# A long-convolution gate and two expert layers on one core: weight steps moved later, layer 2 catching up with layer 1, ReLU groups in own banks, and half a transform in three fp32r passes

## The chip, the cores and the metric

The kernel runs on one core of one Trainium2 chip. The metric is the device time of one execution in microseconds (us), as the median of several runs; lower is better. The core has a matrix engine (TensorE, PE), three engines for elementwise work (VectorE = DVE, ScalarE = ACT, GpSimd = POOL), and a sync engine (SP) whose queue here issues most DMAs. Each engine runs its own program in order; semaphores make one wait for another.

## The reference, cut to what matters

```python
def _attn_ref(x, v, pos_emb, w1, w2):          # S = 12480, D = 128
    h_mlp = np.maximum(pos_emb @ w1, 0.0) @ w2
    h_filt = h_mlp * np.exp(-0.01 * np.arange(S))[:, None]
    u, L = x * v, 2 * S
    y = np.fft.irfft(np.fft.rfft(u, n=L, axis=1) * np.fft.rfft(h_filt, n=L, axis=0)[None], n=L, axis=1)[:, :S]
    return x * y

def _moe_ref(x, w_in, w_out):                  # 128 -> 2048 -> 128; the weights come as float64
    r = np.maximum(x @ w_in, 0.0)
    return (r * r) @ w_out

def _moe2_ref(x, w_in, w_out, alpha):
    h = x @ w_in
    return (np.maximum(h, 0.0) + alpha * np.minimum(h, 0.0)) @ w_out

# result: _moe2_ref of _moe_ref of _attn_ref
```

A long convolution (through a Fourier transform of twice the length) makes a gated sequence of 12480 tokens by 128 channels; two expert layers of 2048 hidden units follow, the first with a squared ReLU, the second with a ReLU whose negative side has a slope alpha for each unit.

## The kernel before, in words

**Stages.** The program is one order written out by hand; helper generators yield after each piece, and `run((a, n), (b, m))` interleaves two of them by their counts. In the order of time:

- `z_stage` (4 to 18 us): the filter's ReLU layer. Groups of up to four matmuls fill one PSUM bank (8 blocks of 64 columns, L192); the ReLU with the window factor is done by DVE for a whole group at once (L203) or by ACT block by block (L196). In some groups DVE takes the first half and ACT the second half of the same bank.
- `ar_stage` (19 to 46): the filter's first transform (L229, copies L231, sign flips L214).
- `u_stage(0)` interleaved with `r_stage` (46 to about 120): the signal's transform for the first half of the channels. `u_mm_a(k)` is the first transform (L287, 16 matmuls, two ACT copies L288 out of PSUM); `u_mm_b(k)` the second (L295, L296, L297, L300: four fp32 matmuls of 224 columns; ACT copies one bank at L299; DVE adds and subtracts at L303). There are 16 rounds k, and `u_mm_b(k - 1)` follows `u_mm_a(k)`. `r_stage` (L246, ACT L248, DVE L252 and L253) is the filter's second transform. GpSimd prepares the input of later rounds (L275, L214).
- `u_stage(1)` with `p_stage` (to 190), then the products and the inverse transform (`q0`, `b_stage`, `y_stage`, to 339.75). In these, steps of the weight decoding run beside the transforms.
- `moe` (339.75 to the end): both expert layers.

**Expert layers.** A table `seq` of 800 steps holds (layer, chunk of tokens, block t of 128 hidden units): 25 chunks (23 of 512 tokens, 2 of 352) by 16 blocks by 2 layers. At step k of one loop the program issues: `up(k)`, three fp32r matmuls into one of four banks (`mm3`, L582 to L584: high and low halves of both operands); `act(k)`, for layer 1 a ReLU on ACT (L602), for layer 2 either DVE's min times alpha (L607) or, at every third step, two ACT instructions (L604, L605); `mid(k - 1)` on DVE (L617), which reads the bank for the last time; `high(k - 2)`, ACT's cast to fp32r (L624); `low`, the remainder, on GpSimd, or on DVE at every fourth step (L635); and `down(k - 6)`, three more matmuls (L582 to L584 again) that add into the chunk's output bank. Layer 2 of a chunk needs all 16 steps of layer 1; its input is split into halves in `split_x`.

**Weights of layer 2.** They come as 64-bit words and are decoded in parts of two blocks. `decode` is a generator of 7 steps a part: load to `s_w` (L489, on SP's queue, three parts ahead), ACT (L495, L465), DVE or GpSimd (L453 to L470). `moe(back)` calls `next(back)` inside its loop, so each weight step is put into the engines' programs at one place of one step k. Weights decoded earlier come back from DRAM (`w_spill`) by POOL's queue into `w_o0b` and `w_i` (L775, L776).

Of the kernel before, what the change touches and what calls it, by code (L numbers as in the profile page):

```python
# [21 lines left out]
KA = HA + 1  # L22
# [36 lines left out]
def kernel(  # L59
# [122 lines left out]
        return w1_sb, win_sb  # L182

    def z_stage(w1_sb, win_sb):
        n_g = -(-HZ // 4)
        for g in range(n_g):
            j0 = 4 * g
            m = min(4, HZ - j0)
            n = min(2 * m, HB - 2 * j0)
# [3 lines left out]
            z = rv[:, :, 0, 2 * j0:2 * j0 + n]  # L193
            c = 0 if g in (1, 5, 9) else n // 2 if g in (3, 7, 11, 13) else n
            for i in range(c, n):
                nc.scalar.activation(  # L196
                    out=z[:, :, i],
                    in_=p[:, i],
                    func=ACTF.Relu,
                    scale=win_sb[:, 2 * j0 + i:2 * j0 + i + 1],  # L200
                )
            if c:
                nc.vector.scalar_tensor_tensor(  # L203
                    out=z[:, :, :c].rearrange("p f t -> p t f"),
                    in0=p[:, :c],
                    scalar=0.0,
                    in1=win_sb[:, 2 * j0:2 * j0 + c].unsqueeze(2).to_broadcast([NA, c, F]),
                    op0=ALU.max,
                    op1=ALU.mult,
                )  # L210
            yield

    def signed(eng, out, src, m):
        eng.tensor_tensor(out=out, in0=src, in1=sig_sb.unsqueeze(1).to_broadcast([NA, m, HB]), op=ALU.mult)  # L214

    def ar_stage():
        def turn(c):
            if c < F // 4:
                f = rv[:, 4 * c:4 * c + 4]
                signed(nc.vector if c < 2 else nc.gpsimd, f[:, :, 1], f[:, :, 0], 4)  # L220

        for c in range(4):
            turn(c)
        for c in range(F // 4):
            f0 = 4 * c
            p = [bank(r_any, HB, 4, K2) for s in range(2)]
# [51 lines left out]

    a_t = {}

    def u_mm_a(k):
        q, u = (t[:NA, :, 0:HB] for t in xv_ring[k % NV])
        a_t[k] = [a_ring[k % 2][i][:HB].rearrange("p d (c k) -> p d c k", c=2) for i in range(2)]
        for s, y in enumerate((u, q)):
            p = bank(r_a, HB, DG, 2, KA)
            for d in range(DG):
                nc.tensor.matmul(p[:, d], lhsT=y[:, d], rhs=dfa[:, s])  # L287
            nc.scalar.copy(out=a_t[k][s], in_=p)  # L288

    def u_mm_b(k):  # L290
# [226 lines left out]
    def in_place(key):  # L517
        return lambda t, n: w[key][0][0][:, :, t:t + n]
# [57 lines left out]
    def moe(back):  # L576
# [113 lines left out]
    PIN, POUT = "p (t k) -> p t k", "(t p) k -> p t k"  # L690

    with tc.manual_schedule():
        wst = ctx.enter_context(tc.tile_pool(name="wst", bufs=1))
        decode = weights(wst)
        back = decode([
            (moe_w_in, PIN, in_place("i0"), 0, NT, nc.gpsimd),
            (moe_w_out, POUT, lambda t, n: spill_w(0, t, n), ONE, NT, nc.gpsimd),
            (moe2_w_in, PIN, lambda t, n: spill_w(1, t, n), 0, SPILL, nc.gpsimd),
            (moe_w_out, POUT, in_place("o0"), 0, ONE, nc.gpsimd),
        ])  # L700
        with ExitStack() as st:
            late = st.enter_context(tc.tile_pool(name="late", bufs=1))
            w2_sb = late.tile([128, 2 * D], F32, name="w2_sb")
            dfa = late.tile([NA, 2, K2], F32, name="dfa")
            sig_sb = late.tile([NA, HB], F32, name="sig_sb")
            r_ring = ring_of(late, 3, [128, 2, 4, HB], F32, "r")
            with tc.tile_pool(name="early", bufs=1) as early:
                run((z_stage(*load_first(early)), 1))
                run((ar_stage(), 1))
            with tc.tile_pool(name="rt", bufs=1) as rt:  # L710
                run((u_stage(0), 2 * NG), (r_stage(rt, r_ring), KP))
            (wide,) = last_two("wide", 1024)
            r_b.items, r_h.items, r_ab.items = six[2:4], six[4:6], six[0:4]
            big = st.enter_context(tc.tile_pool(name="tt", bufs=1))
# [33 lines left out]
        def pairs(pool, n, dtype, name):  # L748
            return [tuple(pool.tile([128, CH], dtype, name=f"{name}{i}{j}") for j in range(2)) for i in range(n)]
# [16 lines left out]
        x2_ring += pairs(p_m, OFF // NT + 2, F32R, "x2")  # L766
# [5 lines left out]
        nc.sync.dma_start(out=alpha, in_=moe2_alpha.rearrange("(t p) -> p t", p=128))  # L772
# [47 lines left out]
def _tables(cell):  # L820
    f = np.float32
    p = np.arange(S, dtype=np.float32)
    w = np.concatenate([np.exp(-0.01 * p), np.zeros(1, np.float32)])
    th = 2 * np.pi * ((np.arange(NA)[:, None] * np.arange(KA)) % NA) / NA
    sn = np.sin(th)
    sn[:, [0, HA]] = 0.0
    dft_a = np.stack([np.concatenate([np.cos(th), i * sn], 1) for i in (-1, 1)], 1).astype(f)
# [12 lines left out]
    return w[cell].astype(f), dft_a, dft_b, e.astype(f), np.stack([o, -o], 1).astype(f)  # L840
# [59 lines left out]
```

## Time and profile before

| | us |
|---|---|
| median of 3 runs | 1418.62 (1418.13 to 1418.75) |
| the profiled execution | 1417.81 |
| its span in the trace | 1416.0 |
| PE busy | 1395.9 (99%) |
| DVE busy | 1118.8 (79%) |
| POOL busy | 1005.9 (71%) |
| ACT busy | 979.3 (69%) |

The span is what the trace records, 1.8 us less than the time of that execution. Busy times are sums over the instructions of an engine; a matmul's end is modelled and overlaps the next one, so the spacing of the starts is the better measure of what one costs.

### The profile page before, as it was taken

The page shows a single profiled execution, that of the slowest core. Times are in us where ns is not written, and L with a number is a line of the kernel's source. Part 1 is how long each engine was busy: PE and PEld are TensorE (multiplying, and loading weights), DVE is VectorE, ACT ScalarE, POOL GpSimd, SP SyncE. Part 2 cuts the span into 40 slices and gives each one's busy share as a digit, 9 for nine tenths or more (in the row PEclk, how much of TensorE's full clock was granted, in tenths as well). Part 3 has the DMA queues.
Part 4 walks back from the last instruction along what each step waited for, and adds up shares of the span by engine and source line. Part 5 has one row for each costly group of instructions (what it writes and reads, how often), then busy time and mean ns, then how long its engine had stood idle before and what let it go on. Part 6 is the DMA issues. An engine that isn't in the chain of part 4 may idle for free.

```text
span 1416.0 us, 22790 instructions
## 1 busy us (share of the span) xinstructions
PE 1395.9 (99%) x7598; PEld 1213.0 (86%) x7598; DVE 1118.8 (79%) x1795; ACT 979.3 (69%) x1851; POOL 1005.9 (71%) x838
## 2 busy tenths in 40 slices
PE   9999989998999999999999999999999999999998
PEld 9999979998888888888888888888888888888888
DVE  4456899886878887878777777877787777788998
ACT  4444322723888787777787777777787777787777
POOL 4944856544877877777777777777777777776776
PEclk9999999999999999999999999999999999999999
DMA  7566324297100000000000000000000000000000
GB/s 206 158 185 188 104 69 121 80 263 235 38 16 1 0 8 9 8 8 1 9 8 8 9 0 9 8 8 8 1 9 8 8 9 8 1 9 8 16 8 19
DMA packets 59018, 66.20 MB, mean 47 GB/s; under 512 B 6226, under 2 KB 48019, under 8 KB 58771
## 3 DMA queue, kind: packets, MB, share of 16 engines
q1 hardware_dynamic: 57802, 60.60, 14.4%
q0 software_dynamic: 688, 3.93, 0.8%
q8 instruction: 60, 0.98, 0.3%
q14 instruction: 59, 0.48, 0.1%
q10 hardware_dynamic: 409, 0.21, 0.1%
HBM read 47.81 MB, written 16.92 MB: 46 GB/s over the span
## 4 chain that ended last, share of the span: by engine, by line
PE 77%; ACT 1%; POOL 1%; DVE 1%; issue 1%; DMA 0%; POOLq 0%; SPq 0%; DVEq 0%; ACTq 0%
PE bank L582 18%; PE bank L584 18%; PE bank L583 18%; PE pair L583 6%; PE pair L584 6%; PE pair L582 6%; PE bank L422 2%; PE bank L423 2%; POOL g L635 1%; ACT G L377 1%; DMA s_w<-in_moe_w_out_dram 0%; ACT pair L495 0%; DVE R L617 0%; ACT w_i L465 0%; DVE pair L453 0%
## 5 line engine op out<-in xcount | busy, mean ns | idle before, releaser
L635 POOL TENSOR_TENSOR g<-R,g 128x512 fp32r<-128x512 f32 (+1 forms) x598 | 778.7, 1322 | 261.2 <-ACT g L624 233.4
L617 DVE SCALAR_TENSOR_TENSOR R<-bank,e 128x512 f32<-128x512 f32 (+1 forms) x800 | 531.0, 674 | 157.9 <-POOL g L635 101.9
L624 ACT CAST g<-R 128x512 fp32r<-128x512 f32 (+1 forms) x800 | 468.8, 605 | 46.3 <-DVE R L617 34.4
L602 ACT ACTIVATE e<-bank 128x512 f32<-128x512 f32 (+1 forms) x400 | 234.9, 587 | 140.1 <-PE bank L584 137.3
L607 DVE TENSOR_SCALAR e<-bank,alpha 128x512 f32<-128x512 f32 (+1 forms) x266 | 194.9, 733 | 34.1 <-PE bank L584 33.4
L635 DVE TENSOR_TENSOR g<-R,g 128x512 fp32r<-128x512 f32 (+1 forms) x202 | 167.0, 827 | 0.0
L583 PE MATMUL pair<-g,w_o 128*128 128x512 f32 (+1 forms) x400 | 153.7, 384 | 0.6 <-DVE g L635 0.3
L582 PE MATMUL bank<-x,w_i 128*128 128x512 f32 (+1 forms) x400 | 153.8, 384 | 0.1
L583 PE MATMUL bank<-x,w_i 128*128 128x512 f32 (+1 forms) x400 | 153.6, 384 | 0.0
L584 PE MATMUL pair<-g,w_o 128*128 128x512 f32 (+1 forms) x400 | 153.6, 384 | 0.0
L584 PE MATMUL bank<-x,w_i 128*128 128x512 f32 (+1 forms) x400 | 153.6, 384 | 0.0
L582 PE MATMUL pair<-g,w_o 128*128 128x512 f32 (+1 forms) x400 | 153.6, 384 | 0.0
L582 PE MATMUL bank<-g,w_o0b 128*128 128x512 f32 (+1 forms) x350 | 134.4, 384 | 0.0
L584 PE MATMUL bank<-g,w_o0b 128*128 128x512 f32 (+1 forms) x350 | 134.3, 384 | 0.0
L583 PE MATMUL bank<-g,w_o0b 128*128 128x512 f32 (+1 forms) x350 | 134.3, 384 | 0.0
L604 ACT ACTIVATE e<-bank 128x512 f32<-128x512 f32 (+1 forms) x134 | 78.8, 588 | 31.9 <-PE bank L584 30.8
L605 ACT ACTIVATE e<-e,alpha 128x512 f32<-128x512 f32 (+1 forms) x134 | 95.6, 714 | 4.4
L583 PEld LDWEIGHTS pair<-g,w_o 128*128 128x128 f32 x400 | 75.1, 188 | 15.4 <-DVE g L635 0.6
L584 PEld LDWEIGHTS bank<-x,w_i 128*128 128x128 f32 x400 | 75.1, 188 | 14.4
L584 PEld LDWEIGHTS pair<-g,w_o 128*128 128x128 f32 x400 | 75.1, 188 | 14.4
L582 PEld LDWEIGHTS bank<-x,w_i 128*128 128x128 f32 x400 | 75.1, 188 | 14.2 <-DVE R L617 0.9
L582 PEld LDWEIGHTS pair<-g,w_o 128*128 128x128 f32 x400 | 75.1, 188 | 14.1
(126 smaller groups left out, 2517.2 us busy)
## 6 DMA issues: line engine op xcount, KB each, us to landing
r<-spill SPq DMA_DIRECT2D x22, 460.0 KB, 3.2
G<-in_xs_dram SPq DMA_DIRECT2D x32, 224.0 KB, 3.5
G<-in_vs_dram SPq DMA_DIRECT2D x32, 224.0 KB, 3.7
spill<-r SPq DMA_DIRECT2D x14, 460.0 KB, 3.0
out_dram<-R SPq DMA_DIRECT2D x23, 256.0 KB, 2.0
R<-in_xt_dram SPq DMA_DIRECT2D x27, 218.0 KB, 4.3
s_w<-in_moe_w_in_dram SPq DMA_DIRECT2D x16, 256.0 KB, 3.9
s_w<-in_moe_w_out_dram SPq DMA_DIRECT2D x16, 256.0 KB, 2.9
```

The lines of the kernel that those rows point to most:

```text
L422: nc.tensor.matmul(pv, lhsT=le, rhs=re, start=True, stop=False)
L423: nc.tensor.matmul(pv, lhsT=lo, rhs=ro, start=False, stop=True)
L582: nc.tensor.matmul(p, lhsT=wl, rhs=xh, start=first, stop=False)
L583: nc.tensor.matmul(p, lhsT=wh, rhs=xl, start=False, stop=False)
L584: nc.tensor.matmul(p, lhsT=wh, rhs=xh, start=False, stop=last)
L602: nc.scalar.activation(out=r, in_=p, func=ACTF.Relu)
L604: nc.scalar.activation(out=r, in_=p, func=ACTF.Relu, scale=-1.0)
L605: nc.scalar.activation(out=r, in_=r, func=ACTF.Copy, scale=alpha[:, t:t + 1])
L607: nc.vector.tensor_scalar(out=r, in0=p, scalar1=0.0, scalar2=alpha[:, t:t + 1], op0=ALU.min, op1=ALU.mult)
L617: nc.vector.scalar_tensor_tensor(out=g, in0=p, scalar=0.0, in1=r, op0=ALU.max, op1=op)
L624: nc.scalar.copy(out=gh, in_=g)
L635: eng.tensor_tensor(out=gl, in0=g, in1=gh.bitcast(F32), op=ALU.subtract)
```

## The change

It has five parts.

1. *Weight steps.* `next(back)` was called at every k not divisible by 3, from k = 1. Now it is called at k = 2 (which only issues the first loads) and at every k from 16 on. The load of `alpha` goes from ahead of the loop to k = 16.
2. *Order of the two layers.* `seq` had layer 2 start 80 steps after layer 1 and then alternate with it, so that it had the last 80 steps alone. Now it starts after 81 steps, comes a little oftener than layer 1 (374 to 320), and has the last 26 steps alone. In these ACT takes two of five of layer 2's activations, and DVE every eighth remainder.
3. *ReLU groups.* Each group belongs to one engine and has a bank of its own: nine times four matmuls for DVE and two for ACT, then a short end.
4. *Second transform of the first half.* Both the tables and the first transform's result are split into a high fp32r half (ACT) and a low one (DVE), and three fp32r products (low x high, high x low, high x high) of 448 columns for each of the two outputs take the place of the four fp32 matmuls of 224 columns. The second half (`u_stage(1)`) stays as it was.
5. *Pools.* The weight decoder's tiles are made after `u_stage(0)`, and some tiles lie on the other side of the memory.

```diff
-    OFF = 4 * NT
+    AHEAD, BEHIND = 5 * NT, 26
...
-        if j < n and (i >= j + NT + OFF or i == n):
+        while j < n and (i == n or j * (n - AHEAD) < (i - AHEAD) * (n - BEHIND)):
             seq.append((1, j // NT, j % NT))
             j += 1
+    ALONE = len(seq) - BEHIND
...
         def on_act(k):
-            return k % 3 == 1
+            return k % 5 in (1, 3) if k >= ALONE else k % 3 == 1
...
         def on_dve(k):
-            return k % 4 == 0 or k >= len(seq) - 2
+            return k % (8 if k >= ALONE else 4) == 0 or k >= len(seq) - 2
...
-            if k % 3:
+            if k == 2 or k >= NT:
                 next(back, None)
+            if k == NT:
+                nc.sync.dma_start(out=alpha, in_=moe2_alpha.rearrange("(t p) -> p t", p=128))
...
-        for g in range(n_g):
...
-            c = 0 if g in (1, 5, 9) else n // 2 if g in (3, 7, 11, 13) else n
...
+        for m, eng in [(4, nc.vector), (2, nc.scalar)] * 9 + [(2, nc.vector), (1, nc.scalar), (1, nc.vector)]:
...
+    def u_mm_a3(k, parts):
+        q, u = (t[:NA, :, 0:HB] for t in xv_ring[k % NV])
+        a_t[k] = parts()
+        for s, (y, o) in enumerate(((u, 0), (q, K2 + KA))):
+            p = bank(r_a, HB, DG, 2, KA)
+            for d in range(DG):
+                nc.tensor.matmul(p[:, d], lhsT=y[:, d], rhs=dfa[:, o:o + K2])
+            hi, lo = (t[:, :, s] for t in a_t[k])
+            src = p.rearrange("p d c k -> p c d k")
+            nc.scalar.copy(out=hi, in_=src)
+            nc.vector.tensor_tensor(out=lo, in0=src, in1=hi.bitcast(F32), op=ALU.subtract)
+
+    def u_mm_b3(k):
+        hi, lo = a_t.pop(k)
+        ps = [bank(r_b, HB, 2, DG, KA) for _ in range(2)]
+        t = t_ring[k % 2][:HB].rearrange("p d (c k) -> p c d k", c=2)
+        for eo in (1, 0):
+            th, tl = (tab[:, eo] for tab in df3)
+            for i, (w, x) in enumerate(((th, lo), (tl, hi), (th, hi))):
+                nc.tensor.matmul(ps[eo], lhsT=w, rhs=x[:, eo], start=i == 0, stop=i == 2)
+            if eo:
+                nc.scalar.copy(out=t, in_=ps[1])
+        u = U(0, 2 * DG * k, 2 * DG).rearrange("p (d s) (c k) -> p s c d k", s=2, c=2)
+        for s, op in enumerate((ALU.add, ALU.subtract)):
+            nc.vector.tensor_tensor(out=u[:, s], in0=ps[0], in1=t, op=op)
```

The first place is ACT's program where the expert layers begin (`e` are the activations, `bank` the four PSUM banks of `up`, `g` the high halves; `pair0<-s_w0` is the first weight instruction). Before:

```order
L602 ACTIVATE e0_2728<-bank0_69 128x512
L602 ACTIVATE e1_2729<-bank1_70 128x512
L602 ACTIVATE e2_2730<-bank2_71 128x512
L624 CAST g00_2700<-R2_82 128x512
L495 ACTIVATE pair0_1965<-s_w0_95 128x256
L602 ACTIVATE e0_2728<-bank3_72 128x512
L624 CAST g10_2702<-R2_82 128x512
L602 ACTIVATE e1_2729<-bank0_69 128x512
```

The same place of the changed program (L625 is the former L602, L647 the former L624):

```order
L625 ACTIVATE e0_2797<-bank0_69 128x512
L625 ACTIVATE e1_2798<-bank1_70 128x512
L625 ACTIVATE e2_2799<-bank2_71 128x512
L647 CAST g00_2769<-R2_82 128x512
L625 ACTIVATE e0_2797<-bank3_72 128x512
L647 CAST g10_2771<-R2_82 128x512
L625 ACTIVATE e1_2798<-bank0_69 128x512
L647 CAST g20_2773<-R2_82 128x512
```

The weight instruction on `s_w0` is gone from between the first cast and the fourth ReLU; the first one now comes after step 16.

The second place is SP's queue at the same point. Before:

```order
L772 DMA alpha_2731<-in_moe2_alpha_dram 128x16x1
L489 DMA s_w0_95<-in_moe2_w_out_dram 128x2x128
L489 DMA s_w1_96<-in_moe2_w_out_dram 128x2x128
L489 DMA s_w2_97<-in_moe2_w_out_dram 128x2x128
```

The same in the changed program (L511 is the former L489):

```order
L511 DMA s_w0_1073<-in_moe2_w_out_dram 128x2x128
L511 DMA s_w1_1074<-in_moe2_w_out_dram 128x2x128
L511 DMA s_w2_1075<-in_moe2_w_out_dram 128x2x128
L713 DMA alpha_2800<-in_moe2_alpha_dram 128x16x1
```

The load of alpha has moved behind the first three weight loads.

The third place is one round of `u_stage(0)` on PE (`pair` and `bank5` rows are `r_stage`; `dfa` is the first transform's table, `dfb` the second's). Before:

```order
L287 MATMUL bank0_69<-dfa_106,G_80 115x112 x4
L287 MATMUL bank1_70<-dfa_106,G_80 115x112 x4
L246 MATMUL pair1_79<-dfb_86,R2_82 128x115 x4
L295 MATMUL bank2_71<-G_80,dfb_86 115x4x56
L296 MATMUL bank4_73<-G_80,dfb_86 115x4x56
L297 MATMUL bank2_71<-G_80,dfb_86 115x4x56
L300 MATMUL bank4_73<-G_80,dfb_86 115x4x56
```

The same round in the changed program (`xh`, `xl` are the high and low halves of the first transform's result, `df30`, `df31` those of the table):

```order
L283 MATMUL bank0_69<-dfa_96,G_80 115x112 x4
L283 MATMUL bank1_70<-dfa_96,G_80 115x112 x4
L242 MATMUL pair1_79<-dfb_86,R2_82 128x115 x4
L296 MATMUL bank4_73<-xl0_444,df30_439 115x448
L296 MATMUL bank4_73<-xh0_443,df31_440 115x448
L296 MATMUL bank4_73<-xh0_443,df30_439 115x448
L296 MATMUL bank3_72<-xl0_444,df30_439 115x448
L296 MATMUL bank3_72<-xh0_443,df31_440 115x448
L296 MATMUL bank3_72<-xh0_443,df30_439 115x448
```

Four matmuls have become six, all of one bank's together; their inputs `xh0`, `xl0` come from the first transform of the round before, since `xh1`, `xl1` are made from the `bank0` and `bank1` shown here.

## Rows read from the trace of the kernel before

**Rows 1.** The page, part 1: busy time of each engine, share and instructions.

```profile
PE 1395.9 (99%) x7598; PEld 1213.0 (86%) x7598; DVE 1118.8 (79%) x1795; ACT 979.3 (69%) x1851; POOL 1005.9 (71%) x838
```

**Rows 2.** Waits of PE, 0 to 360 us: us in total, times, longest us.

```profile
PE bank L346 <- DVE T L351: 5.4, 8, 1.8
PE bank L582 <- DVE R L617: 4.6, 1, 4.6
...
PE bank L229 <- issue: 1.7, 1, 1.7
```

**Rows 3.** Windows: from:to, length, busy PE PEld DVE ACT POOL, clock, DMA.

```profile
46.00:119.00 73.00, 73.00 (x599) 71.94 (x598) 35.36 (x84) 34.53 (x74) 44.63 (x39) 1.00 0.62 186
...
190.00:254.00 64.00, 57.93 (x504) 54.13 (x503) 62.73 (x76) 16.08 (x30) 43.05 (x42) 1.00 0.29 86
...
355.00:450.00 95.00, 95.00 (x421) 78.65 (x420) 75.13 (x135) 82.98 (x161) 75.57 (x58) 1.00 0.06 17
450.00:1250.00 800.00, 800.00 (x3538) 662.87 (x3537) 638.57 (x960) 632.39 (x1138) 611.20 (x461) 1.00 0.02 7
...
1380.00:1411.00 31.00, 30.41 (x183) 29.11 (x181) 29.61 (x60) 24.70 (x55) 22.26 (x23) 1.00 0.04 16
```

**Rows 4.** Waits of the whole span, then the timeline at 19.5 us.

```profile
DVE G L203 <- ACT G L196: 2.8, 4, 0.8
...
19.54 0.42 PE L229 MATMUL bank<-dfa,G 110*115 110x112 f32 x2 [1.66 <-issue]
```

**Rows 5.** Timeline at 88 and 1255 us; by form, DVE, 46 to 119.

```profile
88.31 0.54 PE L295 MATMUL bank<-G,dfb 115*115 115x224 f32 x2
...
88.69 0.54 PE L296 MATMUL bank<-G,dfb 115*115 115x224 f32 x2
...
1254.86 0.39 PE L583 MATMUL bank<-x,w_i 128*128 128x512 f32 x1
...
1255.09 0.39 PE L584 MATMUL bank<-x,w_i 128*128 128x512 f32 x1
...
L303 DVE TENSOR_TENSOR G<-bank,G 115x448 f32<-115x448 f32 x29 | 16.8, 620 | 13.7 <-ACT G L299 13.7
```

**Rows 6.** The chain of waits, 338 to 350 us: start, us, what.

```profile
340.01 0.38 SPq L772
...
340.44 6.77 DMA s_w<-in_moe_w_out_dram
...
347.24 0.41 ACT pair L495
...
347.67 0.43 DVE pair L453
348.10 0.60 DVE R L617
```

**Rows 7.** Timeline at 344 and 354, a window, and a DMA's time to landing.

```profile
343.73 0.39 PE L584 MATMUL bank<-xa,w_i 128*128 128x512 f32 x1
...
354.46 0.39 PE L582 MATMUL bank<-g,w_o0b 128*128 128x512 f32 x1
...
349.00:353.50 4.50, 4.50 (x11) 3.52 (x12) 3.59 (x7) 3.27 (x7) 3.92 (x3) 0.51 1.12 443
...
w_o0b<-w_spill POOLq DMA_DIRECT2D x1, 512.0 KB, 6.3
```

**Rows 8.** Groups by form, DVE, 355 to 450 us: busy, mean ns.

```profile
L617 DVE SCALAR_TENSOR_TENSOR R<-bank,e 128x512 f32<-128x512 f32 x69 | 47.1, 687 | 17.2 <-POOL g L635 16.0 <-ACT e L602 0.2
...
L635 DVE TENSOR_TENSOR g<-R,g 128x512 fp32r<-128x512 f32 x17 | 14.4, 845 | 0.0
```

**Rows 9.** Groups by form, DVE, 1380 to 1411 us.

```profile
L617 DVE SCALAR_TENSOR_TENSOR R<-bank,e 128x352 f32<-128x352 f32 x31 | 15.7, 517 | 1.4 <-POOL g L635 1.1
...
L607 DVE TENSOR_SCALAR e<-bank,alpha 128x352 f32<-128x352 f32 x20 | 11.5, 575 | 0.0
...
L635 DVE TENSOR_TENSOR g<-R,g 128x352 fp32r<-128x352 f32 x9 | 6.8, 759 | 0.0
```

More of the change, by code (lines that the diff above doesn't have):

```diff
@@ L184, in z_stage @@
     def z_stage(w1_sb, win_sb):
-        n_g = -(-HZ // 4)
-        for g in range(n_g):
-            j0 = 4 * g
-            m = min(4, HZ - j0)
-            n = min(2 * m, HB - 2 * j0)
+        j0 = 0
+        for m, eng in [(4, nc.vector), (2, nc.scalar)] * 9 + [(2, nc.vector), (1, nc.scalar), (1, nc.vector)]:
+            b0, b1 = 2 * j0, min(2 * (j0 + m), HB)
             p = bank(r_any, NA, 2 * m, F)
@@ L192, in z_stage @@
                 nc.tensor.matmul(p[:, 2 * i:2 * i + 2], lhsT=posv[:, j0 + i], rhs=w1_sb)
-            z = rv[:, :, 0, 2 * j0:2 * j0 + n]
-            c = 0 if g in (1, 5, 9) else n // 2 if g in (3, 7, 11, 13) else n
[L195 to L202, printed above, removed]
+            if eng is nc.scalar:
+                for b in range(b0, b1):
+                    nc.scalar.activation(
+                        out=rv[:, :, 0, b], in_=p[:, b - b0], func=ACTF.Relu, scale=win_sb[:, b:b + 1]
+                    )
+            else:
                 nc.vector.scalar_tensor_tensor(
-                    out=z[:, :, :c].rearrange("p f t -> p t f"),
-                    in0=p[:, :c],
+                    out=rv[:, :, 0, b0:b1].rearrange("p f t -> p t f"),
+                    in0=p[:, :b1 - b0],
                     scalar=0.0,
-                    in1=win_sb[:, 2 * j0:2 * j0 + c].unsqueeze(2).to_broadcast([NA, c, F]),
+                    in1=win_sb[:, b0:b1].unsqueeze(2).to_broadcast([NA, b1 - b0, F]),
                     op0=ALU.max,
@@ L210, in z_stage @@
                 )
+            j0 += m
             yield
+        assert j0 == HZ
     def signed(eng, out, src, m):
@@ L228, in ar_stage @@
                 for j in range(4):
-                    nc.tensor.matmul(p[s][:, j], lhsT=rv[:, f0 + j, s], rhs=dfa[:, s])
+                    nc.tensor.matmul(p[s][:, j], lhsT=rv[:, f0 + j, s], rhs=dfa[:, s * K2:(s + 1) * K2])
             for s, copy in enumerate((nc.scalar.copy, nc.vector.tensor_copy)):
@@ L286, in u_mm_a @@
             for d in range(DG):
-                nc.tensor.matmul(p[:, d], lhsT=y[:, d], rhs=dfa[:, s])
+                nc.tensor.matmul(p[:, d], lhsT=y[:, d], rhs=dfa[:, s * K2:(s + 1) * K2])
             nc.scalar.copy(out=a_t[k][s], in_=p)
@@ L303, in u_mm_b, with u_stage @@
             nc.vector.tensor_tensor(out=u[:, :, s], in0=pe, in1=t, op=op)
-    def u_stage(h):
+    def u_stage(h, parts=None):
         for k in range(h * NG, (h + 1) * NG + 1):
@@ L309, in u_stage @@
                 load(k + NV - 1)
-                u_mm_a(k)
+                u_mm_a3(k, parts) if parts else u_mm_a(k)
                 yield
             if k > h * NG:
-                u_mm_b(k - 1)
+                u_mm_b3(k - 1) if parts else u_mm_b(k - 1)
                 yield
@@ L686, in moe @@
                 down(k - LAG)
-            if k % 3:
+            if k == 2 or k >= NT:
                 next(back, None)
+            if k == NT:
+                nc.sync.dma_start(out=alpha, in_=moe2_alpha.rearrange("(t p) -> p t", p=128))
     PIN, POUT = "p (t k) -> p t k", "(t p) k -> p t k"
     with tc.manual_schedule():
[L693 to L700, printed above, removed]
         with ExitStack() as st:
-            late = st.enter_context(tc.tile_pool(name="late", bufs=1))
+            late = st.enter_context(tc.tile_pool(name="late", bufs=1, side="right"))
             w2_sb = late.tile([128, 2 * D], F32, name="w2_sb")
-            dfa = late.tile([NA, 2, K2], F32, name="dfa")
+            dfa = late.tile([NA, 2 * K2 + KA], F32, name="dfa")
             sig_sb = late.tile([NA, HB], F32, name="sig_sb")
@@ L710 @@
             with tc.tile_pool(name="rt", bufs=1) as rt:
-                run((u_stage(0), 2 * NG), (r_stage(rt, r_ring), KP))
+                df3 = [rt.tile([HB, 2, HB], F32R, name=f"df3{i}") for i in range(2)]
+                tab = dfb[:, 0:2, :HB]
+                nc.scalar.copy(out=df3[0], in_=tab)
+                nc.vector.tensor_tensor(out=df3[1], in0=tab, in1=df3[0].bitcast(F32), op=ALU.subtract)
+                halves = Ring(
+                    [rt.tile([HB, 2, 2, DG, KA], F32R, name=f"x{n}{i}") for n in "hl"] for i in range(2)
+                )
+                run((u_stage(0, halves), 2 * NG), (r_stage(rt, r_ring), KP))
+            wst = ctx.enter_context(tc.tile_pool(name="wst", bufs=1))
+            decode = weights(wst)
+            back = decode([
+                (moe_w_in, PIN, in_place("i0"), 0, NT, nc.gpsimd),
+                (moe_w_out, POUT, lambda t, n: spill_w(0, t, n), ONE, NT, nc.gpsimd),
+                (moe2_w_in, PIN, lambda t, n: spill_w(1, t, n), 0, SPILL, nc.gpsimd),
+                (moe_w_out, POUT, in_place("o0"), 0, ONE, nc.gpsimd),
+            ])
             (wide,) = last_two("wide", 1024)
             r_b.items, r_h.items, r_ab.items = six[2:4], six[4:6], six[0:4]
-            big = st.enter_context(tc.tile_pool(name="tt", bufs=1))
+            big = st.enter_context(tc.tile_pool(name="tt", bufs=1, side="right"))
             tt = ring_of(big, 2, [HB, D, 2, 4], F32, "T")
@@ L765 @@
         g_ring += pairs(p_m, LAG + 2, F32R, "g")
-        x2_ring += pairs(p_m, OFF // NT + 2, F32R, "x2")
+        x2_ring += pairs(p_m, AHEAD // NT + 1, F32R, "x2")
         e_ring += [
@@ L771 @@
         p_m.tile([128, TOP - NT], F32, name="top_m")
-        nc.sync.dma_start(out=alpha, in_=moe2_alpha.rearrange("(t p) -> p t", p=128))
         cuts = [ONE, ONE + 4, NT]
@@ L826, in _tables @@
     sn[:, [0, HA]] = 0.0
-    dft_a = np.stack([np.concatenate([np.cos(th), i * sn], 1) for i in (-1, 1)], 1).astype(f)
+    dft_a = np.concatenate([np.cos(th), -sn, np.cos(th), sn, np.cos(th)], 1).astype(f)
     ph = 2 * np.pi * ((np.arange(HB)[:, None] * np.arange(HB)) % NB) / NB
```

## Prediction

> **What bounds the kernel now.** I read the engine shares first [rows 1]: TensorE (PE) is busy 99% of the span, so the time is that of PE's instructions plus the few places where PE stands still. The stage windows [rows 3] say the same with one exception. PE is busy 73.00 of 73 us in the first half's transform, all of 355 to 450 and of 450 to 1250, and 30.41 of 31 in the last steps; only in 190 to 254 is it not the bound (57.93 of 64, while VectorE, DVE, has 62.73). So a gain has two forms here: fewer or cheaper PE instructions in a stage where PE is full, or a PE stall that goes. The waits of PE [rows 2] list the stalls: 5.4 us over 8 waits in the DVE-bound stage, one of 4.6 us on L582 at the start of the expert layers, and 1.7 us ahead of the first L229. Edits on other engines are worth only what they do to these. The profiled execution took 1417.81 us, the median of the runs is 1418.62: I sum against the first and add 0.8 at the end.
>
> **Start of the expert layers.** The chain [rows 6] shows what the 4.6 us are. On SP's queue the alpha load (340.01) stands ahead of the s_w loads (340.44); the first s_w takes 6.77 us to land; then the decode step's ACT instruction (347.24, 0.41), its DVE instruction (347.67, 0.43), and behind it L617 (348.10), which frees the bank that PE waits for. The weight step was put in ACT's program ahead of the fourth ReLU and in DVE's ahead of the fourth L617, so both engines stood still for a load that nothing in these steps needs. The changed ACT program has no weight instruction there until step 16; the three s_w loads are still issued at step 2, and alpha follows them, 65 steps before layer 2 reads it. The stall goes, and with it a second loss: after it PE runs 4.50 us at a granted clock of 0.51 [rows 7], the lower level (1.2 of 2.4 GHz). The two together are read off one instruction. The first product with w_o0b starts at 354.46 [rows 7] and is the 16th matmul after the last one ahead of the stall, whose start is 343.73 [rows 7]. At the full-clock spacing of 0.23 us [rows 5], more finely 800 us / 3538 = 0.226 [rows 3] with some records missing, I take 0.2275, that is 343.73 + 16 x 0.2275 = 347.4, or 7.1 us earlier. What must keep up: the ACT work of steps 3 and 4 starts when step 0's is done, at about 343.2, and needs 0.6 a piece; w_o0b's first part is issued at 340.30 and lands after 6.3 [rows 7], at 346.6, 0.8 ahead of its use. I take **-7.0**; bounds -7.1 (nothing new waits) and -3 (w_o0b or GpSimd's L635 takes its place for half the stall and the clock falls again).
>
> The 56 weight steps (8 parts of 7) then run at every step from 16 to 71 instead of at two of three. A layer-1 step costs PE 6 x 0.2275 = 1.365 us. DVE's share is L617 0.687, a quarter of L635's 0.845 [rows 8] and one weight instruction of 0.43 [rows 6]: 1.33. It fits, with 0.03 to spare, and DVE's instructions overlap a little at their ends. Cost taken: 0. If the cover were gone, each 0.1 us over 1.365 would cost 5.6 us (rival D).
>
> **First half's second transform.** Before, each of 16 rounds has four fp32 matmuls of 224 columns; the spacing is 88.69 - 88.31 = 0.38 for a pair of records [rows 5], so 1.52 a round. After, six fp32r matmuls of 448 columns. The trace has no such matmul; the nearest is the expert layers' 512 columns at 0.2275, and by columns 448/512 of it is 0.20, so 1.20 a round. 16 x 0.32 = 5.1 less. From below, half the old matmul's 0.38 is 0.19 and gives 6.1; from above, 448 columns as dear as 512 gives 16 x (1.52 - 1.365) = 2.5. The Trainium skill ("TensorE: Matmul & The Clock Gate", Back-to-back issue gap) gives the warm gap of an isolated matmul as columns/2.4 ns plus 2.5, so an estimate of 189 ns for 448 and 6.2 us for the whole; for 512 it gives 216 ns where this trace has 227, so I keep the row's price.
>
> The new hi/lo split is hidden work: the ACT copy stays one per 448 columns (now with an fp32r output), and DVE gains 32 subtractions from PSUM. Their nearest row is L303, 620 ns at the same size [rows 5]: 19.8 us. DVE is busy 35.36 of 73 [rows 3], so it comes to 55.2 in 68, 81%; PE stays the bound. What is queued behind a late subtraction on DVE is r_stage's L252/L253 and the next L303. In PE's program the six matmuls of a round come after the next round's first transform, so the split has nearly a round to be ready: 4.9 us before (the window of 73 us holds 15 rounds, two L303 each, of which 29 are recorded), 4.6 after. The tables' split, done once, adds an ACT and a DVE instruction of 230 columns ahead of the stage, about 0.4 each: taken as 0.3. Term: **-4.8**; bounds -1.5 (half of the low end is lost to DVE) and -6.1.
>
> **ReLU groups.** Before, DVE waits 4 times, 2.8 us, for ACT in the same bank at L203 [rows 4], and PE 1.66 us before L229 [rows 4] for the stage to end. After, ACT and DVE never share a bank, and DVE's last group is one block of 64 columns instead of three. The matmuls are the same. The end should come near PE's own last matmul, so about half of the 1.66 goes: **-0.9**; bounds 0 (the loads of L229's operands or the signs set the start) and -1.7.
>
> **Catching up.** Layer 2 starts after 81 steps and takes 374 steps while layer 1 takes 320; it is alone in the last 26, before in 80. All 4800 products of the two layers stay. In the mixed part DVE's mean step is 0.687 + 0.25 x 0.845 + 0.54 x 2/3 x 0.74 = 1.17 against PE's 1.365 (the 0.74 is 0.575 [rows 9] with the 352 columns brought to 512 as L617 does, 0.517 to 0.687); half of the steps were layer 2 before, so +0.02. Alone, with 352 columns, PE's step is about 0.95 (0.2275 x 352/512 x 6). DVE's was 2/3 x 0.575 + 0.517 + 0.25 x 0.759 = 1.09 [rows 9] and becomes 0.6 x 0.575 + 0.517 + 0.125 x 0.759 = 0.96, near balance. So DVE was behind in the last 80, yet [rows 3] show PE idle for 0.6 us there: the six-step lag absorbs most of it. Term: **-0.6**; bounds -0.6 and +2 (ACT, with more of the work, falls behind in the last 26 by 0.08 a step).
>
> The weight tiles' and the right-hand pools' new places move no instruction that PE waits for in the program order: 0.
>
> **Sum**: -7.0 - 4.8 - 0.9 - 0.6 = -13.3; 1417.81 - 13.3 = 1404.5, and 0.8 more for the median: **1405.3 us**.
>
> **Rivals.**
> A. *A new wait at the start of the expert layers.* Alpha's load no longer delays s_w, so 768 KB of s_w run beside w_o0b; the 0.8 us margin above is all there is. If w_o0b is 2 to 4.7 us late, PE waits there instead, and the clock falls again: 1407.3 to 1410. For it: its landing already took 6.3 us. Against: before, the same loads ran beside it.
> B. *The split binds the first-half transform.* ACT reads a bank, then DVE reads it and ACT's result, and only then may PE refill it. If this chain, DVE at 81% with it, lengthens each round by 0.3 us, the gain of the passes is gone: 1405.3 + 4.8 = 1410.1. Against: copy 0.53 and subtraction 0.62 of a 4.6 us round. The Trainium skill ("PSUM — Partial Sum Buffer", PSUM bank collisions raise a hardware error) says two engines may not access one bank at once even when both read, so the copy and the subtraction can't overlap; the four L203 waits of [rows 4] are what such an order costs in this trace.
> C. *Time saved early is lost again in the DVE-bound stage* (190 to 254), if its loads or DVE, not what comes before, set its end: 0.9 + 4.8 lost, 1411.0. Against: the stage starts when its inputs do, and is shifted whole.
> D. *Slower.* Weight steps at every step overfill DVE or ACT between steps 16 and 71. From 0.24 us over 1.365 a step on, 56 steps eat all 13.3; at 0.3 they cost 16.8: 1405.3 + 16.8 = 1422.1. For it: 1.33 summed on DVE. Against: DVE is 75.13 busy of 95 [rows 3] with two weight instructions in three steps; a third of 0.43 more per 1.365 makes 90%.
> E. *No net change.* The mixed part lengthens by 13.3/694 = 0.019 us a step, because pairs of layer-2 steps come back to back: about 1418. Against: PE 800.00 of 800 with DVE at 638.57 [rows 3].
>
> **Numbers.** Forecast 0.64 (its own range 1402.3 to 1407.3), A 0.13, B 0.09, C 0.06, D 0.04, E 0.04. The low end is all lower bounds, 7.1 + 6.1 + 1.7 + 0.6 = 15.5, from 1417.81; the high end takes in A to C: range **1402.3 to 1411.0**, which leaves out D, E and mixtures. A measurement here tells about 0.2%, 2.8 us, from no change: faster below 1415.8 is the forecast and A to C, 0.92; same is E, 0.04; slower is D, 0.04.
>
> **What would show it.** Right: no wait of PE on L582's successor over 1 us after 340, a granted clock near 1 from there on, and 7 us between the two kernels in the step of the first w_o0b product; fp32r spacing of 0.20 and rounds of about 4.6 instead of 4.9; no waits of DVE for ACT in the first 18 us; PE full from step 16 to 71. Wrong: a PE wait for a DMA or GpSimd near 346; rounds still at 4.9 with PE waiting for the split; DVE above 95% in steps 16 to 71 with PE waiting for L617.

## The result, and the profile after

| | before | after |
|---|---|---|
| median, us | 1418.68 (4 runs, 1418.13 to 1420.64) | 1402.95 (4 runs, 1402.77 to 1404.29) |
| profiled execution, us | 1417.81 | 1402.77 |
| its span, us | 1416.0 | 1401.0 |

The ratio of the times is 0.9889, 95% interval 0.9872 to 0.9906: 15.7 us faster. The forecast was 1405.3, within 1402.3 to 1411.0.

In the changed kernel the line numbers are 23 higher in the expert layers, 4 lower up to the first half's transform, and 22 higher from the second half's on: L605 to L607 are the former L582 to L584, L625 L602, L640 L617, L647 L624, L658 L635, L287 is the new subtraction; the second half's first transform, which shared L287 before, is L309, and the last transform's L422 is L444. The page's first part:

```profile
PE 1389.3 (99%) x7566; PEld 1205.7 (86%) x7566; DVE 1158.4 (83%) x1824; ACT 977.8 (70%) x1850; POOL 1006.9 (72%) x841
```

PE's busy time falls by 6.6 us against [rows 1] and the span by 15, so by this count more than half of the gain is idle time. (A matmul of 512 columns counts as busy for 0.39 us at full clock and for 0.63 at half clock behind the stall, so the split is rough.) The waits of PE over the whole span (us in total, times, longest us) show which:

```profile
PE bank L368 <- DVE T L373: 3.7, 7, 1.8
PE bank L444 <- ACT G L399: 1.4, 1, 1.4
...
PE pair L225 <- ACT G L193: 0.6, 1, 0.6
```

The 4.6 us on the former L582 [rows 2] are gone, and the 1.7 us ahead of the first L229 are 0.6 now (L225). The timeline gives the first matmul of each stage:

```profile
18.19 0.45 PE L225 MATMUL pair<-dfa,G 110*115 110x112 f32 x2 [0.61 <-ACT G L193]
...
44.56 1.17 PE L283 MATMUL bank<-dfa,G 110*115 110x112 f32 x10
...
115.46 0.76 PE L309 MATMUL bank<-dfa,G 110*115 110x112 f32 x6
...
277.72 0.44 PE L444 MATMUL bank<-ide,G 112*128 112x55 f32 x2 [1.39 <-ACT G L399]
...
331.94 0.48 PE L605 MATMUL bank<-xa,w_i 128*128 128x512 f32 x1
...
339.53 0.39 PE L605 MATMUL bank<-g,w_o0b 128*128 128x512 f32 x1
```

Before, the same instructions start at 19.54, 45.86, 121.61, 284.01, 339.75 and 354.46. So the 15.0 us of the two spans divide exactly:

| stretch | before | after | difference | forecast |
|---|---|---|---|---|
| to the first half's transform | 45.86 | 44.56 | -1.30 | -0.9 |
| first half's transform | 75.75 | 70.90 | -4.85 | -4.8 |
| second half, products, inverse | 162.40 | 162.26 | -0.14 | 0 |
| last transform | 55.74 | 54.22 | -1.52 | 0 |
| first expert matmul to first w_o0b product | 14.71 | 7.59 | -7.12 | -7.0 |
| from there to the end | 1061.54 | 1061.47 | -0.07 | -0.6 |

Two rows of it were not forecast well, the fourth and the last; the experiments are mostly about these and about what made the fifth. Busy times by window (as [rows 3]):

```profile
44.56:115.46 70.90, 70.46 (x578) 67.91 (x577) 57.81 (x120) 35.54 (x77) 45.23 (x39) 1.00 0.64 192
...
331.90:354.00 22.10, 22.04 (x98) 17.73 (x97) 16.02 (x25) 18.78 (x37) 17.89 (x15) 1.00 0.56 182
354.00:430.00 76.00, 76.00 (x336) 62.66 (x335) 66.86 (x129) 67.09 (x134) 59.84 (x46) 1.00 0.06 18
```

The first half's transform stays PE-bound with DVE at 57.81 of 70.9 (82%; 81% was forecast). At the start of the experts PE is busy 22.04 of 22.1 at full clock. In the stretch with a weight step at every step DVE is at 88% (90% forecast).

### The profile page after: what moved, and what is told of

It is laid out like the page before. It is cut to its first block, busy times and chain, and to the rows that moved or that the text cites. A ratio compares the mean times of both kernels' runs of the same rounds, so it can differ in the third digit from the quotient of the medians.

```text
span 1401.0 us, 22648 instructions
## 1 busy us (share of the span) xinstructions
PE 1389.3 (99%) x7566; PEld 1205.7 (86%) x7566; DVE 1158.4 (83%) x1824; ACT 977.8 (70%) x1850; POOL 1006.9 (72%) x841
## 4 chain that ended last, share of the span: by engine, by line
PE 79%; ACT 1%; POOL 1%; DVE 1%; issue 0%; POOLq 0%; DVEq 0%
PE bank L605 19%; PE bank L607 19%; PE bank L606 19%; PE pair L606 6%; PE pair L607 6%; PE pair L605 6%; PE bank L444 2%; PE bank L445 2%; ACT G L399 1%; POOL g L658 1%; ACT pair L517 0%; ACT w_i L487 0%; DVE pair L477 0%; DVE f_w L481 0%; DVE pair L475 0%
## 5 line engine op out<-in xcount | busy, mean ns | idle before, releaser
L658 POOL TENSOR_TENSOR g<-R,g 128x512 fp32r<-128x512 f32 (+1 forms) x601 | 779.4, 1314 | 253.5 <-ACT g L647 241.3
L640 DVE SCALAR_TENSOR_TENSOR R<-bank,e 128x512 f32<-128x512 f32 (+1 forms) x800 | 530.1, 672 | 137.4 <-POOL g L658 99.8
L647 ACT CAST g<-R 128x512 fp32r<-128x512 f32 (+1 forms) x800 | 469.8, 605 | 77.5 <-DVE R L640 70.0
L625 ACT ACTIVATE e<-bank 128x512 f32<-128x512 f32 (+1 forms) x400 | 235.0, 587 | 106.6 <-PE bank L607 104.6
L658 DVE TENSOR_TENSOR g<-R,g 128x512 fp32r<-128x512 f32 (+1 forms) x199 | 184.7, 928 | 0.0
L605 PE MATMUL bank<-x,w_i 128*128 128x512 f32 (+1 forms) x400 | 153.8, 384 | 0.0
L605 PE MATMUL pair<-g,w_o 128*128 128x512 f32 (+1 forms) x400 | 153.6, 384 | 0.0
L607 PE MATMUL bank<-x,w_i 128*128 128x512 f32 (+1 forms) x400 | 153.5, 384 | 0.0
L607 PE MATMUL pair<-g,w_o 128*128 128x512 f32 (+1 forms) x400 | 153.5, 384 | 0.0
L605 PE MATMUL bank<-g,w_o0b 128*128 128x512 f32 (+1 forms) x350 | 134.4, 384 | 0.0
L607 PE MATMUL bank<-g,w_o0b 128*128 128x512 f32 (+1 forms) x350 | 134.3, 384 | 0.0
L605 PEld LDWEIGHTS bank<-x,w_i 128*128 128x128 f32 x400 | 75.1, 188 | 15.0 <-DVE R L640 0.9
L606 PEld LDWEIGHTS pair<-g,w_o 128*128 128x128 f32 x400 | 75.2, 188 | 14.8 <-POOL g L658 1.0
L607 PEld LDWEIGHTS bank<-x,w_i 128*128 128x128 f32 x400 | 75.1, 188 | 14.4
L607 PEld LDWEIGHTS pair<-g,w_o 128*128 128x128 f32 x400 | 75.1, 188 | 14.4
L606 PEld LDWEIGHTS bank<-x,w_i 128*128 128x128 f32 x400 | 75.2, 188 | 13.8
```

The source lines that it names most:

```text
L605: nc.tensor.matmul(p, lhsT=wl, rhs=xh, start=first, stop=False)
L606: nc.tensor.matmul(p, lhsT=wh, rhs=xl, start=False, stop=False)
L607: nc.tensor.matmul(p, lhsT=wh, rhs=xh, start=False, stop=last)
L625: nc.scalar.activation(out=r, in_=p, func=ACTF.Relu)
L640: nc.vector.scalar_tensor_tensor(out=g, in0=p, scalar=0.0, in1=r, op0=ALU.max, op1=op)
L647: nc.scalar.copy(out=gh, in_=g)
```

## The experiments

Each kernel is the one before or the changed one with one edit; times are medians, with the ratio to runs of the kernel before on the same chip.

**1 and 2: which half of the weight edit removes the stall.** First the alpha load alone, then the weight steps alone, on the kernel before:

```diff
-        nc.sync.dma_start(out=alpha, in_=moe2_alpha.rearrange("(t p) -> p t", p=128))
...
             if k % 3:
                 next(back, None)
+            if k == NT:
+                nc.sync.dma_start(out=alpha, in_=moe2_alpha.rearrange("(t p) -> p t", p=128))
```

> The kernel before with one edit: alpha is loaded at step 16 of the expert layers instead of ahead of them; the weight steps stay at two of three steps from k = 1. Theory Q (SP's queue is the cause: alpha's load waits for PE's last product of the stage before, and the s_w loads stand behind it): the three s_w loads are issued in the stage before, some 13 us earlier, the weight step at the start finds its data, the stall of 4.6 us and the half clock behind it go, and the time is 1418.7 - 7 = about 1411.7, with the first product of w_o0b about 14.7 - 7.1 = 7.6 to 8.5 us after the first expert matmul. Theory S (the place of the weight step on ACT and DVE is the cause, alpha's place is worth only the 0.43 us of its issue): the stall stays above 3.5 us and the time is 1418 to 1418.7.

```diff
-            if k % 3:
+            if k == 2 or k >= NT:
                 next(back, None)
```

> The kernel before with the other half of the edit: weight steps at k = 2 and at every step from 16, alpha still loaded ahead of the s_w loads. Both theories: no instruction of the first 16 steps waits for s_w, the stall goes, about 1411.7. The rival that w_o0b's first part becomes late beside the s_w loads (which here still start at 340.4): PE waits 0.5 us or more for a DMA at the first product of w_o0b, and its landing takes 6 us or more, against 4.9 in the changed kernel.

Measured: 1413.59, ratio 0.9956 (0.9943 to 0.9968), and 1411.70, ratio 0.9941 (0.9929 to 0.9954). The SP queue and the weight instruction with alpha moved alone (timeline):

```profile
335.10 1.45 SPq L489 DMA_DIRECT2D s_w<-in_moe_w_out_dram  x3
...
343.30 0.40 ACT L495 ACTIVATE pair<-s_w 128x256 f32<-128x256 f32 x1
...
344.81 0.50 PE L582 MATMUL bank<-xa,w_i 128*128 128x512 f32 x1 [0.51 <-DVE R L617]
```

The weight step stands where it stood, at ACT's turn at 343.30, and waits for nothing: its data was asked for at 335.10, ahead of the first expert matmul at 339.94 (5.3 us earlier than before, not 13: the loads of the last transform stand ahead of it on the queue). Theory Q holds and S falls. With the steps moved alone the loads come as late as before:

```profile
340.38 0.38 SPq L772 DMA_DIRECT2D alpha<-in_moe_alpha_dram  x1
340.81 2.43 SPq L489 DMA_DIRECT2D s_w<-in_moe_w_out_dram  x3
...
347.71 0.39 PE L582 MATMUL bank<-g,w_o0b 128*128 128x512 f32 x1
```

and the first w_o0b product still comes 7.6 us after the first expert matmul (340.12), as in the changed kernel, with no wait of PE: w_o0b's first part landed in 5.5 us beside the s_w loads, 4.9 in the changed kernel, 4.6 with alpha moved alone. So each half alone removes the stall, the first but for a rest of 0.5 us; the two don't add. The difference between them is the two early weight instructions: PE waits 0.7 us for L617 with alpha moved alone, and the w_o0b product comes after 8.4 us.

From the first w_o0b product to the end of its span, the second kernel takes 1410.1 - 347.7 = 1062.4 us. By the starts of PE's matmuls that is 0.80 more than before: 0.43 lies in the next 67 matmuls, before any weight step runs, and 0.37 in those from the 300th to the 600th of the experts, in the last of the steps that have one each and just behind them; with alpha moved alone the latter stretch is as before.

**3: the first half's transform back in fp32**, in the changed kernel:

```diff
-                run((u_stage(0, halves), 2 * NG), (r_stage(rt, r_ring), KP))
+                run((u_stage(0), 2 * NG), (r_stage(rt, r_ring), KP))
```

> The changed kernel with the first half's second transform as before (four fp32 matmuls of 224 columns). If the passes are worth what the rounds show (4.61 against 4.90 us, 4.85 over the stage) and nothing later gives it back: 1402.95 + 4.9 = 1407.8, rounds of 4.90. The rival that the stage that VectorE bounds takes back what came early: 1403 to 1404.

Measured 1408.14, ratio 0.9918 (0.9905 to 0.9932). Its stage goes from 44.86 to 120.61 (timeline), 75.75 us as before to the hundredth. The later stage that DVE bounds gave nothing back: rival C falls.

**4: the ReLU groups as before**, in the changed kernel (the old loop of `z_stage`, shown in the diff of the change with a minus).

> The changed kernel with the ReLU groups as before (DVE and ACT share some banks). The forecast's size: 0.9 slower, 1403.9; the size read from the two traces: the first matmul of the first half's transform comes 1.3 us later (45.9 instead of 44.6), 1404.3. The rival that it is hidden by the loads: no change in that start.

Measured 1405.59, ratio 0.9900 (0.9887 to 0.9914). In its profiled execution (1409.68) the granted clock also falls to half in `ar_stage`, which no other profile here shows, and it is at half again in the DVE-bound stage and in the last transform; so I read only the wait ahead of `ar_stage`:

```profile
20.10 0.42 PE L229 MATMUL bank<-dfa,G 110*115 110x112 f32 x2 [1.66 <-issue]
```

The 1.66 us of [rows 4] are back, 0.61 in the changed kernel: 1.05 us for the wait itself. The median is 2.6 us above the changed kernel's, more than either size, and its runs lie 5.5 us apart; the two of them with a mean granted clock of 1.000 took 1404.14 and 1404.63. So the runs don't tell 0.9 from 1.3.

**5: the old order of the two layers**, in the changed kernel (`OFF` as before, `ALONE = len(seq)`).

> The changed kernel with the order of the two layers as before (80 lone steps of layer 2, its shares of ACT and DVE unchanged to the end). The forecast's size: 0.6 slower, 1403.5. By PE's late starts in the last 150 us of the two traces (1.6 against 0.7 us): 0.9 slower, 1403.9. The rival that the lone steps cost what DVE's sum says (1.09 us a step against PE's 0.95, over the 352-column steps): 3 us or more, 1406 and above. The rival that the order is worth nothing: 1402.95.

Measured 1405.55, ratio 0.9906 (0.9893 to 0.9920). The median is 2.6 us above the changed kernel's, but 1.5 of it lies in the last transform, at a granted clock that this edit doesn't touch (window):

```profile
276.00:290.00 14.00, 12.57 (x96) 12.39 (x94) 10.18 (x26) 4.24 (x11) 5.08 (x7) 0.88 0.81 229
```

From the first expert matmul (333.99) to the end of the span (1403.8) it takes 1069.8 us, the changed kernel 1401.0 - 331.9 = 1069.1. The order is worth 0.7 us; the forecast had 0.6. The rival of 3 us and more falls.

**6: two of the three passes**, in the changed kernel:

```diff
-            for i, (w, x) in enumerate(((th, lo), (tl, hi), (th, hi))):
-                nc.tensor.matmul(ps[eo], lhsT=w, rhs=x[:, eo], start=i == 0, stop=i == 2)
+            for i, (w, x) in enumerate(((th, lo), (th, hi))):
+                nc.tensor.matmul(ps[eo], lhsT=w, rhs=x[:, eo], start=i == 0, stop=i == 1)
```

> The changed kernel without one of the three products in each output of the first half's second transform (the table's low half times the data's high half is left out, so the result is less exact); the split on ACT and DVE stays. If PE bounds this stage, 32 matmuls of 0.205 us go: rounds of 4.20 instead of 4.61, 1402.95 - 6.6 = 1396.4. If the split's chain on ACT and DVE is just behind PE (rival B with a smaller margin than forecast), the rounds stay above 4.4 with PE waiting for L287, and the time above 1399.

Measured 1397.26, ratio 0.9851 (0.9838 to 0.9865). One round in the timeline, and the window of the stage:

```profile
78.86 1.77 PE L283 MATMUL bank<-dfa,G 110*115 110x112 f32 x16
...
81.30 0.44 PE L296 MATMUL bank<-xl,df 115*115 115x448 f32 x1
81.58 0.36 PE L296 MATMUL bank<-xh,df 115*115 115x448 f32 x1
81.78 0.36 PE L296 MATMUL bank<-xl,df 115*115 115x448 f32 x1
...
82.18 1.04 PE L242 MATMUL pair<-dfb,R 115*128 115x115 f32 x8
83.06 1.77 PE L283 MATMUL bank<-dfa,G 110*115 110x112 f32 x16
...
44.60:110.00 65.40, 64.82 (x556) 63.17 (x555) 56.05 (x122) 35.27 (x77) 45.02 (x39) 1.00 0.69 211
```

A round is 83.06 - 78.86 = 4.20 us, a pass 0.20, and PE is still full with DVE at 86%. The split's chain is not just behind PE: in rounds 0.4 us shorter it still kept up, so rival B was not near. The stage falls by 6.4 us (6.6 expected), the median by 5.7.

**7: two weight steps at each step from 16**, in the changed kernel:

```diff
-            if k == 2 or k >= NT:
+            for _ in range(1 if k == 2 else 2 if k >= NT else 0):
                 next(back, None)
```

> The changed kernel with two weight steps at each step from 16 (28 steps carry all 56), to see how much room the forecast's 1.33 us on DVE left. By the sum of DVE's rows a step then costs 0.687 + 0.21 + 0.86 = 1.76 us against PE's 1.365: 28 x 0.4 = 11 us slower, 1414, with PE waiting for L640. If the six steps of lag and the overlap at the ends of DVE's instructions absorb part: 1405 to 1412. If DVE was not near its limit: 1402.95.

Measured 1414.72, ratio 0.9967 (0.9954 to 0.9980). Window and wait of PE (300 to 450 us):

```profile
354.00:393.00 39.00, 34.90 (x142) 24.74 (x141) 37.13 (x74) 29.05 (x62) 24.24 (x19) 1.00 0.12 35
...
PE bank L605 <- DVE R L640: 5.0, 6, 1.3
```

DVE is at 95% and PE waits for it; from the first expert matmul (332.26) to the end of the span it is 1078.9 us, 9.9 more than the changed kernel. The sum of DVE's rows said 11. So that sum prices an overfull step about right, as rival D did; two weight steps at every step lie over the limit, and one lies under it, but for the short waits shown below.

**8 and 9: PE kept busy ahead of the last transform**, in the changed kernel and in the one before:

```diff
         flat = ido.rearrange("p s a -> p (s a)")
+        p = bank(r_y, HB, HB)
+        for _ in range(7):
+            nc.tensor.matmul(p, lhsT=cosb, rhs=cosb)
```

> The changed kernel with seven matmuls of 115 columns (1.5 us of PE work that nothing reads) where PE waits 1.4 to 1.7 us at the start of the last transform. In five of the six profiles so far the granted clock is at half for 3.4 us just after this wait, which costs 1.7 us; in the profile of the changed kernel it is not. If PE's idling brings the half clock: full clock from 270 us on in the profile, a median of 1402 to 1403, and no run of 1404 or more that is explained by it. If the fill delays the transform itself: 0.3 or more later, 1403.3 and above. If the half clock has another cause, it stays possible in the profile.

> The kernel before with the same seven matmuls in PE's wait at the start of the last transform. The changed kernel's profile shows that transform 1.5 us shorter than before, which no part of the change touches; the granted clock was at half for 3.41 us in it before. If PE's idling of 1.7 us brings this: the half clock behind it goes, the stretch from the first to the last matmul of the transform falls from 55.7 to about 54.1 us, and the time is 1418.5 - 1.6 = about 1416.9. If it comes from something else (the position in time alone): no change, 1418.5, and the half clock is still there.

Measured: 1403.35 (1402.97 to 1403.45), ratio 0.9894 (0.9878 to 0.9909); and 1417.86, ratio 0.9993 (0.9984 to 1.0002). The windows, of the kernel before, the changed one, the changed one with the fill and the one before with it, a fence for each (the clock is the third number from the end):

```profile
276.00:290.00 14.00, 12.27 (x102) 12.09 (x100) 10.03 (x25) 7.13 (x18) 6.55 (x9) 0.88 0.62 176
```

```profile
276.00:290.00 14.00, 12.61 (x108) 12.43 (x107) 11.27 (x29) 3.81 (x11) 5.82 (x8) 1.00 0.91 261
```

```profile
270.00:290.00 20.00, 20.00 (x183) 19.84 (x182) 15.91 (x40) 9.06 (x23) 9.62 (x14) 1.00 0.73 211
```

```profile
276.00:290.00 14.00, 13.69 (x129) 13.51 (x128) 11.32 (x29) 7.56 (x19) 6.95 (x10) 1.00 0.66 181
```

In the profile of the kernel before with the fill, the half clock is gone, and the last transform from its first own matmul (284.42) to the first expert one (338.65) is 54.23 us instead of 55.74: 1.5 us, the fourth row of the table. That the fill did this is likely but not shown by one profile, since three kernels without a fill are at full clock there too. Whole, that kernel's gain is not told from none: in the profile 0.5 us come back at the expert start (its first w_o0b product 15.2 us after the first expert matmul, 14.7 before), 0.7 behind it, and 0.4 were lost at the very beginning. In the changed kernel the fill changes the median by nothing that can be measured, and there was no half clock for it to take away: the one in the changed kernel's profile lies earlier, in the DVE-bound stage and ahead of the fill (window):

```profile
185.00:205.00 20.00, 16.83 (x117) 15.38 (x116) 19.66 (x29) 2.24 (x5) 12.53 (x17) 0.83 0.15 49
```

It cost little: the second half, products and inverse take 162.26 us in the changed kernel and 162.04 to 162.08 in the four profiles with the same stage at full clock (experiments 3, 5, 6 and 8). In experiment 4, whose half clock there begins 3.6 us later in the stage, they take 164.07. With the fill the four runs lie within 0.5 us at a mean granted clock of 1.000, without it within 1.5 at 0.997 to 0.998; that this is the fill's doing is not shown, as runs of experiments 3 and 4 reached 1.000 without it. Apart from experiment 6, which leaves out a product and is less exact, no kernel here beats the changed one by more than the measurement tells.

## Why the prediction was right, step by step

**Expert start.** Size right (7.1 for 7.0), mechanism half right. I laid the stall on the place of the weight step and counted alpha's load as 0.4 us ahead of the s_w loads. The runs show the queue: alpha's load waits for PE's last product of the last transform, and everything behind it on SP's queue waits too. Before, the chain has these matmuls right ahead of alpha's issue at 340.01 [rows 6]:

```profile
339.75 0.25 PE bank L423 x2
```

The stall needed both, the late loads and an early instruction that waits for them, and either half of the edit ends it. Freed of alpha, the loads go out during the transform; in the changed kernel at 327.10:

```profile
327.10 2.63 SPq L511 DMA_DIRECT2D s_w<-in_moe_w_out_dram  x3
332.20 0.37 SPq L713 DMA_DIRECT2D alpha<-in_moe_alpha_dram  x1
```

The sentence of rival A that the s_w loads would now run beside w_o0b was therefore wrong, and the rival had less for it than its 0.13: w_o0b's first part landed in 4.9 us, not 6.3 [rows 7]. In experiment 2, where the loads do run beside it, PE didn't wait for it either.

**Weight steps at every step, priced at 0.** This is the step that failed, though by little: 0.8 us more behind the first w_o0b product (experiment 2), in two parts, and I had priced both at nothing. The later 0.37 is not 0.03 us a step used up: it is two single late starts of PE. In the changed kernel:

```profile
412.04 1.16 DVE L658 TENSOR_TENSOR g<-R,g 128x512 fp32r<-128x512 f32 x1
...
413.87 0.39 PE L607 MATMUL bank<-g,w_o0b 128*128 128x512 f32 x1
...
414.52 0.39 PE L606 MATMUL bank<-xb,w_i 128*128 128x512 f32 x1
...
428.74 0.41 DVE L492 TENSOR_TENSOR w_o<-pair,m_w 128x256 fp32r<-128x256 f32 x1
...
434.20 1.17 DVE L658 TENSOR_TENSOR g<-R,g 128x512 fp32r<-128x512 f32 x1
...
435.87 0.39 PE L607 MATMUL bank<-g,w_o0b 128*128 128x512 f32 x1
...
436.55 0.39 PE L606 MATMUL bank<-xa,w_i 128*128 128x512 f32 x1
```

From 413.87 to 414.52 and from 435.87 to 436.55 lie two spacings, which at 0.2275 make 0.455: PE is 0.20 and 0.23 late, each time behind a remainder of 1.16 or 1.17 us on DVE, where the mean was 0.845 [rows 8]. The second place comes after DVE's last weight instruction (428.74). In the kernel before and in experiment 1 no start there is more than 0.1 late. Why these remainders take longer, and how much of the 0.37 the weight instructions make, stays open.

The earlier 0.43 comes in steps without any weight instruction; the changed kernel's timeline shows it too:

```profile
340.94 1.41 DVE L658 TENSOR_TENSOR g<-R,g 128x512 fp32r<-128x512 f32 x1
...
342.45 1.89 DVE L640 SCALAR_TENSOR_TENSOR R<-bank,e 128x512 f32<-128x512 f32 x3
...
342.74 0.40 PE L607 MATMUL bank<-g,w_o0b 128*128 128x512 f32 x1
343.20 0.50 PE L605 MATMUL bank<-xa,w_i 128*128 128x512 f32 x1
```

Three L640 stand behind a remainder of 1.41 us on DVE, and PE starts 0.23 late at 343.20 and some more at the matmuls beside it. All nine profiles without the stall have this loss of about 0.4, the two with it (the kernel before and experiment 9) have none. That the other engines had caught up with PE there, while it stood still, fits this. The order's gain of 0.7 (experiment 5; the sum had 0.6) hid both parts: together -0.07, where I had -0.6.

**First half's transform.** Right in size, with parts that differ: passes of 0.20 by columns, measured 0.205 in the rounds and 0.20 in experiment 6; rounds of 4.61 us. One round of the timeline, with the split beside it:

```profile
82.16 1.77 PE L283 MATMUL bank<-dfa,G 110*115 110x112 f32 x16
...
83.16 0.53 ACT L286 CAST xh<-bank 115x448 fp32r<-115x448 f32 x1 [0.41 <-PE bank L283]
...
83.73 0.62 DVE L287 TENSOR_TENSOR xl<-bank,xh 115x448 fp32r<-115x448 f32 x1 [0.24 <-ACT xh L286]
...
84.59 0.44 PE L296 MATMUL bank<-xl,df 115*115 115x448 f32 x1
84.87 0.57 PE L296 MATMUL bank<-xh,df 115*115 115x448 f32 x2
85.28 0.37 PE L296 MATMUL bank<-xl,df 115*115 115x448 f32 x1
...
85.89 1.04 PE L242 MATMUL pair<-dfb,R 115*128 115x115 f32 x8
...
86.77 1.77 PE L283 MATMUL bank<-dfa,G 110*115 110x112 f32 x16
```

The first of the six passes takes 0.28, so they take 1.30 a round (84.59 to 85.89), not 1.20: they save 0.22 of the 0.32 forecast. Another 0.08 a round, which I had not counted, comes from `r_stage`'s matmuls just ahead of them (0.82 us, 0.90 before).

The cast ends, then the subtraction starts, 0.04 us later: ACT and DVE read the bank one after the other. That order costs PE no time here, because the matmuls that use the result belong to the next round. The Trainium skill ("PSUM — Partial Sum Buffer", PSUM bank collisions raise a hardware error) says that two engines may not read one bank at the same time. The trace agrees but is no test of it: the subtraction also reads the cast's result, and so has to follow it anyway.

The Trainium skill's gap for an isolated matmul ("TensorE: Matmul & The Clock Gate", Back-to-back issue gap) gave an estimate of 189 ns. The trace has 205, nearer to the row's price of 0.20.

**ReLU groups.** 1.3 for 0.9: the wait fell by 1.05, nearly two thirds of 1.66 where I took half, and DVE no longer waits for ACT in the first 18 us (2.8 us before). The other 0.3 is not shown to be the edit's: the first half's transform starts at 44.55 to 45.25 us in the six profiles with the new groups (the changed kernel, experiments 3 and 5 to 8) and at 45.86 to 46.29 in the four of the kernel before and its edits, by their means 1.2 apart.

**What no step had.** The last transform, 1.5 us, at the granted clock: half for part of it before, full in the changed kernel's profile. It is not an effect of the change that I can show: with the same wait of 1.4 us ahead of it, three kernels (experiments 3 to 5) were at half clock there and three (the changed one, 6 and 7) were not. The three profiles with the 1.7 us of before and no fill (the kernel before, experiments 1 and 2) all were, so it isn't excluded that the shorter wait makes it less likely. Without it the profiled difference is 13.5, against 13.3 forecast. So that the result came 2.4 us below the forecast, close to the low end of its range, was for the most part luck; 0.6 more is the step from profile to median, 0.8 before and 0.2 after.

Rivals A to E: none occurred. A is refuted by experiment 2, B by 6, C by 3; D's mechanism exists, and at two weight steps a step it costs 9.9 us (7); E's loss in the mixed part is less than the order's gain (5).

## What to carry to other kernels

A DMA that must wait for an engine should not stand at the head of a queue with loads behind it that could go now; look at what is queued behind a waiting issue before blaming the instruction that waits for the data. Two edits that remove the same stall don't add, so try each alone. An engine that fits a step on average with 2% to spare can still be late where its work bunches, here by 0.4 us in 56 steps and just behind them: don't price it at zero.

## What the runs showed of the hardware

A wait of PE of 1.4 to 1.7 us at the start of the last transform was followed by a granted clock of half (1.2 of 2.4 GHz) for 3.4 us in six of nine profiled kernels, worth 1.5 us, and not in the other three. With unused matmuls in the wait it was followed by none in two more; one of these, the kernel before, had the half clock without them. What decides between the six and the three stays open, though all three with a wait of 1.7 are among the six. So two profiles of kernels that differ by 1% can differ by 1.5 us in a stage that was not touched. In the stage that DVE bounds, 6.8 us at half clock (0.83 in a window of 20 us) cost the changed kernel only about 0.2 us; with as long a half clock a little later in it, experiment 4 took 2.0 us longer.
